# Seven unread identity products beside the first two chains of a delta-rule and feed-forward kernel, and one fold result evicted sooner

## The chip, the cores and the metric

The kernel runs on one core of one Trainium2 chip. The metric is the device time of one execution in microseconds (us). Engines are named as the profile names them: PE is TensorE's matrix product, PEld its weight load, DVE is VectorE, ACT is ScalarE, POOL is GpSimd, SP is SyncE, which here issues nearly all DMAs. PEclk is the share of TensorE's full clock that was granted.

## The reference

Two blocks follow each other. The first is a delta-rule recurrence over 768 steps for 4 batches of 8 heads of 48 features; the second multiplies its output, as 3072 tokens of 384 features, through four weight matrices with no nonlinearity but one product.

```python
k_n = k / (np.linalg.norm(k, axis=-1, keepdims=True) + 1e-06)
for t in range(S):
    kt, vt, bt = (k_n[:, :, t], v[:, :, t], beta[:, :, t, None])
    y[:, :, t] = np.einsum('bhd,bhde->bhe', q[:, :, t], state)
    v_old = np.einsum('bhde,bhd->bhe', state, kt)
    state = state + bt[:, :, :, None] * np.einsum('bhd,bhe->bhde', kt, vt - v_old)
...
a = x @ w1
b = x @ w2
h = a * b @ w3
return (h @ w_out).astype(np.float32)
```

## The kernel before, in words

The 768 steps are cut into 12 chunks of 64. Inside a chunk the recurrence is a triangular system, and chunks are joined by a state. For a chunk m the parts are, by the names in the order string: `k`, `v`, `p` (loads), `d` (transposes into KQ, lines 320 to 330), `s` (scores, lines 357 to 402: products of KQ with itself, L367 and L373, then on VectorE the scaled system U, L379, and the masked PT, L397), `u` (the 32 by 32 blocks of U are written to DRAM, L414), `e` (the corner, lines 476 to 529: two sets of small products at L498, copies at L514, and the evictions into TT at L525), `c` (the chain, lines 543 to 616: S,KQ, then R on VectorE L584, then R,TT, then X L594, then X,ktok, then the new state S at L613 or L615; all four sets of products have the line L551), and `y` (outputs, lines 619 to 687: products L652, copies into xT L673, DMAs within xT L684).

Two chunks share one inverse `V` (lines 420 to 454): their blocks are read back from DRAM as Ub (L426), and 31 pairs of VectorE instructions (L440, L445) invert them; the result goes out as Vd (L453) and comes back into TT (L462, L469) for the corner. The first two inverses work on a pair of PSUM banks, with two ACT copies in (L434) and out (L449).

The weights arrive as 36 pieces `P` of 64-bit words (their two 32-bit halves are put together into one f32 value). A piece is a load (L699), two ACT activations (L707, L708), two VectorE instructions (L710, L711) and one GpSimd addition (L715), with five raw buffers in turn. w3 and w_out are multiplied into one matrix first: `t` transposes (L750, copy L753), `f` folds (lines 756 to 767: eight products L759, the second half in a second step, and an eviction by ACT at L766). Then `a` and `b` (lines 772 to 796, products L779) make the two hidden factors of 512 tokens, `b` for the first of two chunks only, and `S`, `o`, `x` make the result (L846, L874).

Each part is a Python generator. What it does between two `yield`s is one step, and the order string lists the steps one by one; a name's nth appearance is its nth step. Each engine executes its instructions in the order in which the string issues them:

```python
    for name in ORDER.split():
        step(name)
    in_text_order()
```

Two rings of PSUM matter here. `two_banks` (psW) hands out two pairs of banks in turn, to scores, corners, chains and outputs. `bank` (psF) hands out four single banks in turn, to transposes, folds, `a`, `b`, `o` and a few small ones; a product into a bank waits until the bank's last content has been read.

```python
    def bank(shape):
        return in_turn(psF, shape, "f", 4, "ps_f")
```

Around the change the steps are these, in the string's order: first outputs `y0`, scores `s3` for its second pair of batches, the rest of chain `c0` (X,ktok and the first state), transpose `t13`, corner `e1`, chain `c1` (S,KQ, then R,TT), inverse `V1`, the fold `f6`, outputs `y1`, then `b` and `a`.

Of the kernel before, what the change touches and what calls it, by code (L numbers as in the profile page):

```python
# [54 lines left out]
b0 V1 V1 g2 a04 P34 n2 p4 n2 a07 c1 a04 b2 b4 P33 b6 b2 P35 V1 g2 g2 P34 g2 e2 a07 g2 P33 e2
P35 c2 c2 e3 d4 a03 d4 a03 a01 P33 g2 b4 d4 g2 e2 b6 e2 a07 e2 b4 d4 T a01 T b4 e2 a07 c2 s4 p5
g2 c2 T g2 N2 V2 b6 p5 b6 s4 b5 s4 c2 a06 c2 a06 a04 v3 y2 d5 b5 d5 k6 s4 e3 d5 s4 y2 a02 a05
d5 s4 b7 a04 n3 S0 a02 a05 S0 s5 S0 u4 e3 s5 n3 s5 e3 b7 T o0 c3 c3 s5 g3 s5 S0 N2 N2 x0 e3 g3
e3 o0 s5 c3 c3 u5 o0 x0 V2 S0 x0 y3 V2 y3 S0 V2 S0 V2 S0 S0 V2 V2 V2 S0 g3 o0 S0 o0 S0 x0 V2 c3
o0 v4 y3 V2 V2 V2 x0 p6 V2 x0 V2 S0 a10 a10 S0 g3 S0 x0 V2 x0 S0 o0 x0 x0 p6 a14 V2 k7 a17 a17  # L60
a14 V2 V2 V2 a15 a16 V2 a16 a15 V2 g3 V2 V2 V2 V2 V2 v5 V2 x0 a13 V2 V2 V2 a17 a12 V2 a13 g3 V2
V2 g3 a17 c3 a14 a13 d6 d6 a11 V2 e4 n4 a12 e4 e4 c4 d6 V3 e4 a14 a10 n4 g3 d6 c4 e5 a11 e4 s6
g3 a13 e4 a12 p7 a10 c4 g3 N3 s6 c4 s6 a11 y4 n5 y4 c4 e5 a12 c4 a11 a15 c5 n5 e5 p7 a16 d7 d7
d7 d7 o1 c5 v6 a16 k8 g4 g4 e5 g4 p8 a15 g4 s7 s7 S1 e5 s7 S1 e5 x1 s7 s7 S1 s7 c5 o1 s6 S1 u7
c5 o1 s6 s6 u6 S1 S1 V3 S1 y5 c5 c5 V3 V3 V3 V3 V3 o1 S1 x1 k9 S1 y5 S1 y5 o1 S1 S1 x1 x1 V3 S1
S1 V3 c6 V3 S1 S1 V3 d8 o1 x1 x1 v7 a20 n6 x1 V3 a20 o1 x1 a23 V3 V3 x1 V3 x1 n7 a27 a24 d8 a26
V3 V3 V3 V3 x1 g4 V3 a23 V3 a25 V3 a27 a27 V3 a24 V3 V3 a26 a20 V3 g4 V3 p8 V3 V3 V3 V3 p9 V3
V3 a25 d8 n6 d8 g4 a20 a22 a22 a24 V3 c6 a27 a25 a24 a21 a21 e6 e6 e6 g4 e7 N3 e6 a25 N3 g4 s8
g4 N4 s8 e6 a22 s8 a26 e6 c6 c6 N4 s8 a26 s8 y6 a22 V4 p9 N4 S2 d9 e7 s8 a21 e7 y6 u8 d9 a21 e7
c6 a23 d9 p10 e7 d9 S2 c6 S2 s9 n7 a23 s9 e7 o2 s9 c7 s9 S2 s9 k10 S2 c7 x2 o2 c7 S2 S2 o2 u9  # L70
s9 V4 c7 V4 S2 y7 V4 V4 x2 V4 g5 g5 V4 p10 d10 y7 S2 x2 S2 o2 y7 V4 o2 x2 c7 V4 V4 S2 S2 V4 o2
a35 x2 x2 k11 x2 S2 V4 x2 S2 a35 v8 V4 S2 V4 V4 S2 V4 x2 n8 o2 a37 x2 V4 v9 V4 V4 V4 x2 a34 n8
V4 V4 a36 a30 V4 V4 V4 V4 V4 a37 V4 a34 a33 V4 g5 a33 a30 a32 a36 V4 V4 V4 V4 a34 a33 V4 V5 a32
e8 n9 c7 e8 a30 c8 a33 e8 e9 e8 g5 a35 a34 c8 a30 e8 g5 d10 a32 e9 g5 a32 g5 a36 e8 e9 S3 c8
a36 a35 a31 d10 d10 e9 a31 n9 c8 g5 c8 c8 g5 g5 e9 a31 s10 N5 e9 p11 s10 s10 a31 c9 a37 a37 p11
c9 y8 N5 v11 d11 S3 d11 d11 o3 v10 d11 s10 y8 s10 S3 u10 S3 s11 N5 s11 o3 s10 c9 s11 c9 s11 S3
x3 S3 s11 o3 S3 S3 y9 o3 s11 x3 S3 o3 u11 V5 S3 S3 V5 y9 V5 x3 n11 S3 x3 V5 V5 V5 S3 y9 S3 S3
V5 c9 V5 o3 x3 V5 x3 x3 V5 V5 x3 S3 a47 o3 x3 V5 V5 a47 x3 V5 V5 a47 n10 V5 a46 a40 a40 V5 a47
V5 a43 V5 a46 x3 a42 a45 V5 a42 V5 a41 a45 a43 V5 V5 V5 V5 V5 V5 a44 V5 a44 V5 a45 a41 V5 V5 V5
V5 c9 a42 e10 a40 e10 n11 a42 e10 a44 e10 c10 a45 n10 e11 e10 e11 c10 a43 e10 c10 c10 a40 e11  # L80
a41 a46 e11 c10 a44 S4 a43 e11 a41 S4 c10 o4 e11 a46 c11 x4 S4 S4 y10 o4 c11 c11 S4 y10 S4 S4
S4 S4 S4 c11 o4 y11 o4 x4 S4 S4 S4 o4 y11 x4 x4 o4 S4 x4 x4 S4 y11 S4 x4 x4 a50 x4 o4 a50 x4
a55 a56 a55 a52 a55 a50 a52 a56 a54 a57 a54 a55 a54 a50 a54 a51 a52 a57 a51 a53 x4 a52 a53 a51
a56 a56 a53 a51 a53 a57 o5 S5 a57 S5 S5 o5 S5 S5 S5 x5 S5 S5 S5 o5 o5 x5 S5 S5 S5 o5 S5 S5 S5
# [5 lines left out]
def kernel(  # L90
# [14 lines left out]
    P = 128  # L105
# [43 lines left out]
    def bank(shape):  # L149
        return in_turn(psF, shape, "f", 4, "ps_f")  # L150
# [19 lines left out]
    ident = const.tile([P, P], FP32, name="ident")  # L170
# [361 lines left out]
    xts = {}  # L532

    def scaled_v(c):
        nv = vtoks[c]
        for r in range(NR):
            pool.tensor_tensor(  # L537
                out=nv[:, r], in0=nv[:, r],
                in1=scale_of(ns, c)[:, r].unsqueeze(2).to_broadcast([P, H, D]), op=ALU.mult,
            )  # L540
            yield

    def chain(c):
        TT, nv, KQ = TTs[c % 2], vtoks[c], KQs[c]

        def products(out, lhs, rhs):
            ps = two_banks()
            for r in range(NR):
                for h in range(H):
                    for z in range(2):  # L550
                        pe.matmul(  # L551
                            out(ps, r, h, z), lhsT=lhs(r, h, z), rhs=rhs(r, h, z),
                            start=True, stop=True,
                        )
            return ps[:, :, 0:DM].rearrange("p b (g d) -> p b g d", d=D)


        def crossed(ps, r, h, z):
            g = NP * r + h // 2
            return ps[half((z + h) % 2), h % 2, D * g : D * g + D]  # L560

        def by_tokens_of_features(ps, r, h, z):
            g = NP * r + h // 2
            return ps[half(z), h % 2, D * g : D * g + D]

        def by_features(ps, r, h, z):
# [24 lines left out]
        yield
        Xs[c] = X = in_turn(work, [P, NR, H, D], "X", 2, "X")
        for e in range(2):
            dve.tensor_tensor(  # L594
                out=X[:].rearrange("p r (a e) d -> p e (r a) d", e=2)[:, e], in0=ps[:, e],
                in1=scale_of(ws, c, 1).rearrange("p r (a e) -> p e (r a)", e=2)[:, e]
                .unsqueeze(2).to_broadcast([P, H, D]),
                op=ALU.mult,
            )
        yield  # L600
        if c < NCH - 1:
            kt = ktoks[c]
            ps = products(
                by_features,
                lambda r, h, z: kt[half((z + h) % 2), r, h, :],
                lambda r, h, z: X[half((z + h) % 2), r, h, :],
            )
            yield
            Ss[c + 1] = Sn = in_turn(work, [P, 2, H, D], "S", 2, "S")
            for z in range(2):  # L610
                f = feat(z)
                if c == 0:
                    dve.tensor_copy(out=Sn[f], in_=ps[f])  # L613
                else:
                    dve.tensor_tensor(out=Sn[f], in0=St[f], in1=ps[f], op=ALU.add)  # L615
            yield
# [428 lines left out]
```

## Time and profile before

| | us |
|---|---|
| median of 3 runs | 593.02 |
| lowest and highest | 591.44, 594.95 |
| the profiled execution's own time | 593.18 |
| its span, first to last instruction | 591.5 |
| PE busy | 542.2 (92%) |
| DVE busy | 363.0 (61%) |
| ACT busy | 159.3 (27%) |
| POOL busy | 176.3 (30%) |
| mean granted clock of TensorE | 0.976 |

The span is counted from the first to the last instruction of one execution; its own time has some 1.7 us around that. Busy time is a union: products that overlap in the array count once. The chain that ended last is made of 70% PE, 10% SyncE's queue, 9% DMA and 5% DVE. A wait that the profile lists as "issue" is one in which the engine waited for nothing that the profile shows.

### The profile page before, as it was taken

The page shows a single profiled execution, that of the slowest core. Times are in us where ns is not written, and L with a number is a line of the kernel's source. Part 1 is how long each engine was busy: PE and PEld are TensorE (multiplying, and loading weights), DVE is VectorE, ACT ScalarE, POOL GpSimd, SP SyncE. Part 2 cuts the span into 40 slices and gives each one's busy share as a digit, 9 for nine tenths or more (in the row PEclk, how much of TensorE's full clock was granted, in tenths as well). Part 3 has the DMA queues.
Part 4 walks back from the last instruction along what each step waited for, and adds up shares of the span by engine and source line. Part 5 has one row for each costly group of instructions (what it writes and reads, how often), then busy time and mean ns, then how long its engine had stood idle before and what let it go on. Part 6 is the DMA issues. An engine that isn't in the chain of part 4 may idle for free.

```text
span 591.5 us, 19063 instructions
## 1 busy us (share of the span) xinstructions
PE 542.2 (92%) x8188; PEld 379.8 (64%) x8188; DVE 363.0 (61%) x828; ACT 159.3 (27%) x333; POOL 176.3 (30%) x223
## 2 busy tenths in 40 slices
PE   2569898778999999999999989999999999999997
PEld 2466555657878874558854669645698446974477
DVE  3897898569986579574796545865746924110012
ACT  4666354363412202121210232112121112311100
POOL 7563542033464601207121034111170000600051
PEclk9988999679999999999999999999999999999999
DMA  9989986668856455563553345614432040010001
GB/s 245 196 174 267 199 172 130 120 154 169 140 86 98 98 86 111 78 96 54 124 92 79 46 70 103 127 53 66 59 65 90 13 90 4 17 41 13 1 0 53
DMA packets 219507, 57.31 MB, mean 97 GB/s; under 512 B 206656, under 2 KB 212800, under 8 KB 219424
## 3 DMA queue, kind: packets, MB, share of 16 engines
q1 hardware_dynamic: 215232, 55.31, 46.9%
q10 hardware_dynamic: 4192, 0.79, 1.0%
q8 instruction: 64, 1.05, 0.8%
q14 instruction: 19, 0.16, 0.1%
HBM read 43.88 MB, written 11.01 MB: 93 GB/s over the span
## 4 chain that ended last, share of the span: by engine, by line
PE 70%; SPq 10%; DMA 9%; DVE 5%; issue 2%; ACT 1%; POOL 1%; DVEq 0%; POOLq 0%; ACTq 0%
PE ps_f L779 38%; PE ps_f L874 19%; DMA raw<-in_moe_w_dram 5%; PE ps_w L551 5%; PE ps_w L652 4%; SPq L230 3%; SPq L699 2%; PE ps_w L498 2%; DMA ktok<-in_k_dram 2%; DVE tb L440 1%; SPq L202 1%; DVE ps_w L445 1%; PE ps_w L367 1%; DMA Ub<-Ud 1%; PE ps_w L373 1%
## 5 line engine op out<-in xcount | busy, mean ns | idle before, releaser
L779 PE MATMUL ps_f<-xT,w2s 128*128 128x512 f32 (+1 forms) x336 | 131.8, 538 | 2.1 <-issue 2.1
L779 PE MATMUL ps_f<-xT,w1s 128*128 128x512 f32 (+1 forms) x336 | 128.0, 532 | 2.0 <-DMA xT<-xT 2.0
L846 POOL TENSOR_TENSOR ab<-ab 128x256 f32<-128x256 f32 x96 | 67.0, 727 | 175.3 <-DVE ab L795 153.6
L779 PEld LDWEIGHTS ps_f<-xT,w1s 128*128 128x128 f32 x336 | 63.3, 190 | 57.6 <-issue 52.2
L779 PEld LDWEIGHTS ps_f<-xT,w2s 128*128 128x128 f32 x336 | 62.0, 190 | 55.1 <-issue 51.9
L791 ACT COPY ab<-ps_f 128x512 f32<-128x512 f32 (+1 forms) x56 | 28.2, 526 | 165.8 <-PE ps_f L779 161.7
L874 PE MATMUL ps_f<-w,ab 128*128 128x192 f32 x376 | 66.3, 330 | 0.0
L874 PEld LDWEIGHTS ps_f<-w,ab 128*128 128x128 f32 x376 | 61.2, 190 | 4.2 <-issue 3.3
L795 DVE TENSOR_TENSOR ab<-ab,ps_f 128x512 f32<-128x512 f32 (+1 forms) x56 | 33.1, 603 | 48.9 <-PE ps_f L779 48.7
L440 DVE TENSOR_TENSOR tb<-Vb,Ub 128x31 f32<-128x31 f32 (+15 forms) x124 | 44.7, 360 | 17.2 <-DMA Ub<-Ud 13.9
L874 PE MATMUL ps_f<-room,ab 128*128 128x192 f32 x272 | 48.0, 330 | 0.8 <-DVE room L905 0.8
L445 DVE TENSOR_TENSOR Vb<-Vb,tb 128x31 f32<-128x31 f32 (+15 forms) x124 | 46.0, 371 | 4.3
L759 PE MATMUL ps_f<-w2s,w3T 128*128 128x384 f32 x128 | 45.5, 511 | 0.0
L874 PEld LDWEIGHTS ps_f<-room,ab 128*128 128x128 f32 x272 | 44.1, 190 | 1.6 <-issue 1.1
L673 ACT COPY xT<-ps_w 48x256 f32<-48x256 f32 x96 | 30.5, 366 | 54.4 <-PE ps_w L652 53.9
L270 POOL TENSOR_TENSOR sq<-ktok 128x384 f32<-128x384 f32 x24 | 20.7, 866 | 70.0 <-DMA ktok<-in_k_dram 39.5
L759 PEld LDWEIGHTS ps_f<-w2s,w3T 128*128 128x128 f32 x128 | 25.1, 202 | 16.5 <-issue 2.3
L537 POOL TENSOR_TENSOR vtok<-vtok,n 128x384 f32<-128x384 f32 x24 | 20.3, 859 | 43.1 <-DMA vtok<-in_v_dram 43.1
L367 PE MATMUL ps_w<-KQ 48*64 48x128 f32 x384 | 29.3, 293 | 1.7 <-DVE PT L397 1.7
L373 PE MATMUL ps_w<-KQ 48*64 48x64 f32 x768 | 30.1, 232 | 0.0
L715 POOL TENSOR_TENSOR w<-w,raw 128x512 uint32<-128x512 uint32 x16 | 20.6, 1294 | 29.0 <-issue 7.3
L373 PEld LDWEIGHTS ps_w<-KQ 48*64 48x64 f32 x768 | 27.2, 146 | 0.1
(109 smaller groups left out, 661.0 us busy)
## 6 DMA issues: line engine op xcount, KB each, us to landing
raw<-in_moe_w_dram SPq DMA_DIRECT2D x16, 512.0 KB, 6.5
vtok<-in_v_dram SPq DMA_DIRECT2D x24, 192.0 KB, 4.5
raw<-in_moe_w_dram SPq DMA_DIRECT2D x24, 192.0 KB, 4.7
out_dram<-osb SPq DMA_DIRECT2D x46, 96.0 KB, 2.0
ktok<-in_k_dram SPq DMA_DIRECT2D x44, 96.0 KB, 3.6
raw<-in_moe_w_out_dram SPq DMA_DIRECT2D x8, 384.0 KB, 4.4
Ud<-U SPq DMA_DIRECT2D x48, 64.0 KB, 2.6
Ub<-Ud SPq DMA_DIRECT2D x6, 512.0 KB, 4.1
```

What stands on the lines that cost most here:

```text
L367: pe.matmul(ps[half(z), 0, n : n + 128], lhsT=x[:, 0, :], rhs=x.rearrange("p j t -> p (j t)"), start=True, stop=True,)
L373: pe.matmul(ps[half(z ^ j), 1, n + C * j : n + C * j + C], lhsT=x[:, 0, :], rhs=x[:, j, :], start=True, stop=True,)
L440: dve.tensor_tensor(out=tv, in0=V[:, 0 : s + 1, s : s + 1].to_broadcast([P, s + 1, n]), in1=U[:, s, s + 1 : BS].unsqueeze(1).to_broadcast( ...
L445: dve.tensor_tensor(out=o, in0=o, in1=tv, op=ALU.subtract)
L551: pe.matmul(out(ps, r, h, z), lhsT=lhs(r, h, z), rhs=rhs(r, h, z), start=True, stop=True,)
L673: act.copy(out=xT[f, p:NP:2, b : b + NR, cc, :].rearrange("p a r t -> p r a t"), in_=pyv[f, z, b : b + NR],)
L759: pe.matmul(ps[:, 0:DM], lhsT=w3Ts[jc, kc // 4][:, kc % 4 * P : kc % 4 * P + P], rhs=wo[:, kc], start=(kc == 0), stop=(kc == KF - 1),)
L779: pe.matmul(ps[:].rearrange("p b c t -> p b (c t)"), lhsT=w[:, m, js], rhs=x[:, m, :, c0:c1].rearrange("p b c t -> p b (c t)"), start=(m = ...
L791: act.copy(out=t, in_=ps)
L795: dve.tensor_tensor(out=t, in0=t, in1=ps, op=ALU.mult)
L846: pool.tensor_tensor(out=o_, in0=x_, in1=y_, op=op)
L874: pe.matmul(ps[b][:, b, :], lhsT=abs_[u, HF * f + i][:, t0 : t0 + P], rhs=ws_[w][:, i], start=first and i == 0 and (b == 0 or n == "F"), s ...
```

## The change

A new part `fill` has four steps. It takes one psF bank and writes 2, 1, 1 and 3 products of the identity with four copies of itself side by side (128*128 by 128x512) into it. Nothing reads them. The steps stand behind the products of `y0`, behind the second scores of `s3`, behind the second set of the corner `e1`, and behind S,KQ of chain `c1`.

The third step of `f7`, which evicts fold 7 from its bank, moves from behind the thirteenth step of `V1` to behind the first pieces that follow the corner's first products. Since `fill` takes one bank of the ring, every later bank is the next one in turn.

The look-up of a chunk's v tile moves into the lines that use it, in `scaled_v` and in `chain`; the instructions there stay the same.

```diff
-e1 P26 s2 e1 P25 d3 c0 P21 P30 u2 s3 c0 s3 P26 N1 P31 P24 y0 s3 s3 y0 c0 s3 s3 P25 t13 N1 e1 u3
-P31 c0 P26 P31 P32 c1 V1 c1 e1 P25 V1 P27 c1 V1 c1 V1 V1 t13 V1 V1 V1 V1 V1 V1 y0 V1 P25 f7 f6
+e1 P26 f7 s2 e1 P25 d3 c0 P21 P30 u2 s3 c0 s3 P26 N1 P31 P24 y0 fill s3 s3 fill y0 c0 s3 s3 P25
+t13 N1 e1 fill u3 P31 c0 P26 P31 P32 c1 fill V1 c1 e1 P25 V1 P27 c1 V1 c1 V1 V1 t13 V1 V1 V1 V1
+V1 V1 y0 V1 P25 f6 f6 P30 P32 P32 v2 V1 P27 s1 P31 V1 V1 y1 b3 b1 V1 b0 P32 P28 y1 b1 V1 b1 b3
...
     def scaled_v(c):
-        nv = vtoks[c]
...
     def chain(c):
-        TT, nv, KQ = TTs[c % 2], vtoks[c], KQs[c]
+        TT, KQ = TTs[c % 2], KQs[c]
...
-        R = nv
+        R = vtoks.get(c)
...
+    def fill():
+        ps = bank([P, 4, P])
+        for n in (2, 1, 1, 3):
+            for _ in range(n):
+                pe.matmul(
+                    ps[:], lhsT=ident[:], rhs=ident[:].unsqueeze(1).to_broadcast([P, 4, P]),
+                    start=True, stop=True,
+                )
+            yield
...
+    parts["fill"] = fill
```

More of the change, by code (lines that the diff above doesn't have):

```diff
@@ L49 @@
 N1 P30 t12 t14 t15 e0 t15 d3 f7 d3 f6 e0 P30 P21 e0 e0 P24 f7 s2 s2 e1 e0 s2 P24 e0 e1 V1 p4 s2
-e1 P26 s2 e1 P25 d3 c0 P21 P30 u2 s3 c0 s3 P26 N1 P31 P24 y0 s3 s3 y0 c0 s3 s3 P25 t13 N1 e1 u3
-P31 c0 P26 P31 P32 c1 V1 c1 e1 P25 V1 P27 c1 V1 c1 V1 V1 t13 V1 V1 V1 V1 V1 V1 y0 V1 P25 f7 f6
-f6 P30 P32 P32 v2 V1 P27 s1 P31 V1 V1 y1 b3 b1 V1 b0 P32 P28 y1 b1 V1 b1 b3 P29 P27 b2 b3 y1 V1
-P27 b1 b0 P29 P29 c1 a01 b2 a03 P28 V1 a01 a00 b3 P28 P29 a02 a02 a03 P35 P28 V1 a05 b7 a00 V1
-V1 V1 V1 a06 P33 V1 b5 a05 b7 b0 V1 P34 V1 b5 V1 a06 V1 V1 V1 P34 k4 V1 P35 V1 g2 a00 V1 k5 a00
@@ L55 @@
[L55 to L84, printed above, removed]
@@ L85 @@
-o5 x5 S5 x5 o5 x5 x5 x5 x5 x5 x5 x5 x5 x5 x5
+e1 P26 f7 s2 e1 P25 d3 c0 P21 P30 u2 s3 c0 s3 P26 N1 P31 P24 y0 fill s3 s3 fill y0 c0 s3 s3 P25
+t13 N1 e1 fill u3 P31 c0 P26 P31 P32 c1 fill V1 c1 e1 P25 V1 P27 c1 V1 c1 V1 V1 t13 V1 V1 V1 V1
+V1 V1 y0 V1 P25 f6 f6 P30 P32 P32 v2 V1 P27 s1 P31 V1 V1 y1 b3 b1 V1 b0 P32 P28 y1 b1 V1 b1 b3
+P29 P27 b2 b3 y1 V1 P27 b1 b0 P29 P29 c1 a01 b2 a03 P28 V1 a01 a00 b3 P28 P29 a02 a02 a03 P35
+P28 V1 a05 b7 a00 V1 V1 V1 V1 a06 P33 V1 b5 a05 b7 b0 V1 P34 V1 b5 V1 a06 V1 V1 V1 P34 k4 V1
@@ new lines @@
+P35 V1 g2 a00 V1 k5 a00 b0 V1 V1 g2 a04 P34 n2 p4 n2 a07 c1 a04 b2 b4 P33 b6 b2 P35 V1 g2 g2
+P34 g2 e2 a07 g2 P33 e2 P35 c2 c2 e3 d4 a03 d4 a03 a01 P33 g2 b4 d4 g2 e2 b6 e2 a07 e2 b4 d4 T
+a01 T b4 e2 a07 c2 s4 p5 g2 c2 T g2 N2 V2 b6 p5 b6 s4 b5 s4 c2 a06 c2 a06 a04 v3 y2 d5 b5 d5 k6
+s4 e3 d5 s4 y2 a02 a05 d5 s4 b7 a04 n3 S0 a02 a05 S0 s5 S0 u4 e3 s5 n3 s5 e3 b7 T o0 c3 c3 s5
+g3 s5 S0 N2 N2 x0 e3 g3 e3 o0 s5 c3 c3 u5 o0 x0 V2 S0 x0 y3 V2 y3 S0 V2 S0 V2 S0 S0 V2 V2 V2 S0
+g3 o0 S0 o0 S0 x0 V2 c3 o0 v4 y3 V2 V2 V2 x0 p6 V2 x0 V2 S0 a10 a10 S0 g3 S0 x0 V2 x0 S0 o0 x0
@@ new lines @@
+x0 p6 a14 V2 k7 a17 a17 a14 V2 V2 V2 a15 a16 V2 a16 a15 V2 g3 V2 V2 V2 V2 V2 v5 V2 x0 a13 V2 V2
+V2 a17 a12 V2 a13 g3 V2 V2 g3 a17 c3 a14 a13 d6 d6 a11 V2 e4 n4 a12 e4 e4 c4 d6 V3 e4 a14 a10
+n4 g3 d6 c4 e5 a11 e4 s6 g3 a13 e4 a12 p7 a10 c4 g3 N3 s6 c4 s6 a11 y4 n5 y4 c4 e5 a12 c4 a11
+a15 c5 n5 e5 p7 a16 d7 d7 d7 d7 o1 c5 v6 a16 k8 g4 g4 e5 g4 p8 a15 g4 s7 s7 S1 e5 s7 S1 e5 x1
+s7 s7 S1 s7 c5 o1 s6 S1 u7 c5 o1 s6 s6 u6 S1 S1 V3 S1 y5 c5 c5 V3 V3 V3 V3 V3 o1 S1 x1 k9 S1 y5
+S1 y5 o1 S1 S1 x1 x1 V3 S1 S1 V3 c6 V3 S1 S1 V3 d8 o1 x1 x1 v7 a20 n6 x1 V3 a20 o1 x1 a23 V3 V3
@@ new lines @@
+x1 V3 x1 n7 a27 a24 d8 a26 V3 V3 V3 V3 x1 g4 V3 a23 V3 a25 V3 a27 a27 V3 a24 V3 V3 a26 a20 V3
+g4 V3 p8 V3 V3 V3 V3 p9 V3 V3 a25 d8 n6 d8 g4 a20 a22 a22 a24 V3 c6 a27 a25 a24 a21 a21 e6 e6
+e6 g4 e7 N3 e6 a25 N3 g4 s8 g4 N4 s8 e6 a22 s8 a26 e6 c6 c6 N4 s8 a26 s8 y6 a22 V4 p9 N4 S2 d9
+e7 s8 a21 e7 y6 u8 d9 a21 e7 c6 a23 d9 p10 e7 d9 S2 c6 S2 s9 n7 a23 s9 e7 o2 s9 c7 s9 S2 s9 k10
+S2 c7 x2 o2 c7 S2 S2 o2 u9 s9 V4 c7 V4 S2 y7 V4 V4 x2 V4 g5 g5 V4 p10 d10 y7 S2 x2 S2 o2 y7 V4
+o2 x2 c7 V4 V4 S2 S2 V4 o2 a35 x2 x2 k11 x2 S2 V4 x2 S2 a35 v8 V4 S2 V4 V4 S2 V4 x2 n8 o2 a37
@@ new lines @@
+x2 V4 v9 V4 V4 V4 x2 a34 n8 V4 V4 a36 a30 V4 V4 V4 V4 V4 a37 V4 a34 a33 V4 g5 a33 a30 a32 a36
+V4 V4 V4 V4 a34 a33 V4 V5 a32 e8 n9 c7 e8 a30 c8 a33 e8 e9 e8 g5 a35 a34 c8 a30 e8 g5 d10 a32
+e9 g5 a32 g5 a36 e8 e9 S3 c8 a36 a35 a31 d10 d10 e9 a31 n9 c8 g5 c8 c8 g5 g5 e9 a31 s10 N5 e9
+p11 s10 s10 a31 c9 a37 a37 p11 c9 y8 N5 v11 d11 S3 d11 d11 o3 v10 d11 s10 y8 s10 S3 u10 S3 s11
+N5 s11 o3 s10 c9 s11 c9 s11 S3 x3 S3 s11 o3 S3 S3 y9 o3 s11 x3 S3 o3 u11 V5 S3 S3 V5 y9 V5 x3
+n11 S3 x3 V5 V5 V5 S3 y9 S3 S3 V5 c9 V5 o3 x3 V5 x3 x3 V5 V5 x3 S3 a47 o3 x3 V5 V5 a47 x3 V5 V5
@@ new lines @@
+a47 n10 V5 a46 a40 a40 V5 a47 V5 a43 V5 a46 x3 a42 a45 V5 a42 V5 a41 a45 a43 V5 V5 V5 V5 V5 V5
+a44 V5 a44 V5 a45 a41 V5 V5 V5 V5 c9 a42 e10 a40 e10 n11 a42 e10 a44 e10 c10 a45 n10 e11 e10
+e11 c10 a43 e10 c10 c10 a40 e11 a41 a46 e11 c10 a44 S4 a43 e11 a41 S4 c10 o4 e11 a46 c11 x4 S4
+S4 y10 o4 c11 c11 S4 y10 S4 S4 S4 S4 S4 c11 o4 y11 o4 x4 S4 S4 S4 o4 y11 x4 x4 o4 S4 x4 x4 S4
+y11 S4 x4 x4 a50 x4 o4 a50 x4 a55 a56 a55 a52 a55 a50 a52 a56 a54 a57 a54 a55 a54 a50 a54 a51
+a52 a57 a51 a53 x4 a52 a53 a51 a56 a56 a53 a51 a53 a57 o5 S5 a57 S5 S5 o5 S5 S5 S5 x5 S5 S5 S5
@@ L86 @@
+o5 o5 x5 S5 S5 S5 o5 S5 S5 S5 o5 x5 S5 x5 o5 x5 x5 x5 x5 x5 x5 x5 x5 x5 x5
 """
@@ L534, in scaled_v @@
     def scaled_v(c):
-        nv = vtoks[c]
         for r in range(NR):
             pool.tensor_tensor(
-                out=nv[:, r], in0=nv[:, r],
+                out=vtoks[c][:, r], in0=vtoks[c][:, r],
                 in1=scale_of(ns, c)[:, r].unsqueeze(2).to_broadcast([P, H, D]), op=ALU.mult,
@@ L581, in chain @@
             v3, r3 = (
-                x[:].rearrange("p r (a e) d -> p (r a) e d", e=2) for x in (nv, R)
+                x[:].rearrange("p r (a e) d -> p (r a) e d", e=2) for x in (vtoks[c], R)
             )
```

## The prediction

> **What bounds the kernel now.** I read the page's slices first, for the stage: the change sits between the first two chains, at 108 to 123 us of 591.5.
>
> ```profile
> PE   2569898778999999999999989999999999999997
> PEclk9988999679999999999999999999999999999999
> DMA  9989986668856455563553345614432040010001
> ```
>
> TensorE is nearly full from slice 10 (148 us) to the end. Slices 8 and 9 (103 to 133 us) are the one place after 90 us where its granted clock falls, to 0.7 on average, and the DMA engines are busy there. The second view cuts that stretch along the steps of the clock (us; busy us and count of PE, PEld, DVE, ACT, POOL; PEclk; DMA; GB/s):
>
> ```profile
> 105.85:109.26 3.41, 1.38 (x65) 1.12 (x64) 2.05 (x5) 0.33 (x2) 1.28 (x1) 1.00 0.56 67
> 109.27:112.68 3.41, 3.00 (x104) 2.91 (x108) 1.27 (x3) 2.20 (x8) 0.00 (x0) 0.50 0.86 171
> ...
> 119.51:122.92 3.41, 0.51 (x17) 0.54 (x19) 2.65 (x5) 3.30 (x6) 0.00 (x0) 0.50 0.88 198
> 122.92:126.33 3.41, 3.41 (x62) 2.58 (x57) 1.48 (x3) 1.22 (x3) 2.82 (x3) 0.50 1.01 276
> 126.33:129.74 3.41, 3.36 (x102) 2.17 (x100) 2.17 (x9) 1.50 (x3) 2.16 (x2) 1.00 0.24 45
> ```
>
> The clock is halved at 109.27 us, after a window in which TensorE was busy for 1.38 of 3.41 us (40%), and whole again at 126.33 us: 17.06 us at half. In them TensorE is busy for 11.6 us (3.00 + 2.87 + 1.79 + 0.51 + 3.41, two of the five rows not shown).
>
> The timeline of TensorE shows where it waits (start, length, what; idle before, releaser):
>
> ```profile
> 108.42 0.44 PE L652 MATMUL ps_w<-PT,X 64*48 64x64 f32 x15 [1.45 <-issue]
> ...
> 113.65 1.01 PE L750 MATMUL ps_f<-ident,w 128*128 128x128 f32 x4 [0.54 <-issue]
> 114.59 1.13 PE L498 MATMUL ps_w<-T,T 33*33 33x32 f32 x64
> 115.52 1.92 PE L551 MATMUL ps_w<-S,KQ 48*64 48x48 f32 x59
> 118.18 0.45 PE L551 MATMUL ps_w<-S,KQ 48*64 48x48 f32 x5 [0.75 <-issue]
> 122.41 2.08 PE L551 MATMUL ps_w<-R,TT 64*64 64x48 f32 x64 [3.78 <-ACT TT L525]
> 124.42 3.78 PE L759 MATMUL ps_f<-w2s,w3T 128*128 128x384 f32 x8
> 131.96 3.26 PE L779 MATMUL ps_f<-xT,w1s 128*128 128x256 f32 x14 [0.42 <-DMA xT<-xT]
> ```
>
> What those waits hang on decides the case. The longest, 3.78 us before the products of R and TT, is for the corner's evictions (L525, 120.73 to 121.93). On ScalarE these stand behind an activation of a weight piece, and that behind a DMA. The waits of ACT and DVE in 108 to 128 us:
>
> ```profile
> ACT w2s L707 <- DMA raw<-in_moe_w_dram: 4.3, 1, 4.3
> DVE w2s L710 <- ACT w2s L707: 5.1, 1, 5.1
> DVE tb L440 <- DMA Ub<-Ud: 1.7, 1, 1.7
> ```
>
> The chain of waits says the same of what comes next (start, length, what):
>
> ```profile
> 115.14 1.77 SPq L699
> ...
> 121.11 6.09 DMA Ub<-Ud
> ...
> 158.52 3.06 DMA Vd<-Vb
> ...
> 165.20 0.72 DVE T L481
> ```
>
> SyncE's queue is its own bound: the second block load (Ub) is issued at 121.11 us and lands 6.09 us later; inverse 1 on VectorE (L440, L445) starts then, at 127.29, and through Vd ends at the transpose of 165.20, for which TensorE waits 0.93 us. TensorE itself waits for xT at 131.96 (0.42 us) and at 141.59 (1.63 us, not shown), both DMAs that stand in SyncE's order. So **from 109 to 165 us the pace is set by SyncE's queue, the DMAs and VectorE**; TensorE, although slow, arrives early three times.
>
> [...] the clock is half or whole, [...] 0.50 or 1.00 only, and 17.06 us is five times 3.41. [...] here a window 40% busy was enough, while one 1.81 us busy of 3.41 (53%, 139.99 to 143.40 us) kept the whole clock, and one 1.87 us busy of 3.40 (37.6 to 41.0 us) lost it. The border lies near 53 to 55% by this trace. [...]
>
> **The change part by part.**
>
> *Price of a fill.* One product of 128*128 by 128x512 in f32, whose row has a mean of 538 ns from first to last. In a dense stream what counts is the distance: 60 such products take 25.75 us in the chain (217.67 us), 0.43 each. At half clock I take twice that, 0.86. Seven: 3.0 us at whole clock, 6.0 at half. Their weight loads (190 ns each) run beside them. No shown row has the same identity seven times; 0.43 is the low end and 2 x 0.538 = 1.08 (7.5 us in all) the high one.
>
> *Where they stand.* A, two, after the first outputs (L652, end 108.86), where TensorE idles 0.82 us for a VectorE eviction (L397). B, one, after scores r = 1 of chunk 3, before X,ktok: no idle. C, one, after T,T, before S,KQ: no idle at half clock. D, three, after S,KQ, in the 3.78 us.
>
> *If the clock halves as before* (0.86 each): A is 1.72 less 0.82 = 0.90 late; with B 1.76; with C 2.62: S,KQ ends at 118.63 + 2.62 = 121.25, still before VectorE gets to R at 121.36, which had waited for the piece. D runs to 123.83, so R,TT starts 1.42 us after its 122.41. X (L594) then starts near 125.96 instead of 124.54 and ends near 127.0, before the 127.29 at which inverse 1 starts. R,TT had 1.73 us to spare there and uses 1.42. The fold that follows catches up, since more of it lies after 126.33; outputs 1 end about 0.5 late, against 0.42 + 1.63 us of xT waits ahead. **Cost 0.**
>
> *If A holds the clock at 109.27.* A brings 109.27 - 108.86 = 0.41 us more to the window: 1.79 of 3.41, 52%, just below the border of 53 to 55%. If it holds, scores, X,ktok, T,T and S,KQ shrink by some 4 us and A to D cost 3.0, but R,TT still waits for ACT until about 122.4: S,KQ would be over near 116 and D near 117.3, and the 5 us to 122.4 are over a window long, so the clock halves again at 119.5. R,TT starts when it did; **gain 0**. The cover is SyncE's queue, which asks TensorE for nothing here: u3's scores were evicted at 112.45, its issue came at 117.00.
>
> *The eviction of fold 7* (L766, 0.48 us) moves on ScalarE from 123.68 to about 103.2, ahead of one corner's T copies, the first outputs' copies, two pieces, the TT evictions, two copies of Vb and one transpose's copy. At the new place it pushes the T copies (L514) by 0.48; their reader is T,T at 114.59, and ScalarE has 4.55 us idle behind them. At the old place 4.07 us idle follow. Cost 0. It issues no DMA, and SyncE's and GpSimd's orders are as before.
>
> *Banks.* The fills take one of the four psF banks in turn. transpose 13 comes to fold 7's bank (free at about 103.7, needed at 113.65), b3 to fold 6's (128.72 against 130.40), b0 to the fills' own. Nothing waits; later the distances are as before. The look-ups of vtoks change no instruction.
>
> *Sum.* The profiled execution took 593.18 us (span 591.5 and 1.7 around it); 593.18 + 0. The median shown is 0.16 lower, so 593.0.
>
> **The rivals.**
>
> *Faster: TensorE's clock is the bound.* For it: the chain is 70% PE, PE is busy 92%. Half of the 11.6 us, 5.8, would come back, less what isn't covered of the fills (B and C, 0.9): about 588.3. Against it: the three waits above.
>
> *Slower: R,TT passes its 1.73 us to spare.* X is late, inverse 1 starts late on VectorE, and all up to 165 us moves along. It decides once R,TT starts after about 124.1 us. With seven fills at half clock and none covered, 6.0 - 1.73 = 4.3 us: 597.5. For it: my case at half clock leaves just 0.3 us, and each stall of instruction issue (0.54, 0.75, 1.45 us seen here) can shift. Against it: 3.78 us of cover stand ahead of D.
>
> *It doesn't do what it says:* the clock halves all the same; 593, as worked out.
>
> **How the numbers follow.** The time repeats within 591.44 to 594.95 in the runs shown; 0.5% (3.0 us) is about what can be told from no change. No change by 0.5%: 0.79 (with the clock held or not about evenly). Faster rival, over 3.0 us: 0.13. Slower rival, over 3.0 us: 0.08; small slips of inverse 1 lie inside the 0.79. The range takes the shown spread, plus 1.4 us below for a part of the faster case and 0.6 above for a small slip: 590.0 to 595.6.
>
> **What would show it.** Right: R,TT still ends its wait on ACT L525 near 122.4 or behind the fills near 123.8; inverse 1 starts within 0.3 us of 127.3; TensorE still waits for xT and for T L481 at 165; PE busy rises by about 3 us at most. Wrong: TensorE loses those waits, or Ub is issued at another time than 121 us; the transpose of 165.20 moves by over 1 us.

## The result, and the profile after

The changed kernel takes 600.66 us (median of 4 runs, 599.63 to 604.18) against 593.69 us for the kernel before (4 runs, 591.44 to 594.95): 1.0125 times as long, 95% interval 1.0081 to 1.017. (Here and below, ratios and intervals leave out runs of a slower state, over 1.5% above a kernel's fastest, and are not simply the ratios of the medians.) It is slower by some 7 us, where no change was forecast. Its profiled execution took 599.63 us, with a span of 597.9; the span before was 591.5, so the two traces differ by 6.4 us.

The page of the changed kernel: busy share by slice, granted clock, and the queue that brings instructions (transfers, MB, share):

```profile
PE   2469888897999999999999899999999999999997
PEclk9988999997999999999999999999999999999999
...
q8 instruction: 64, 1.05, 0.7%
```

The fills did their own work. The dip of the clock in slices 8 and 9 (0.6 and 0.7 of full speed there before) is gone; the one slice of 0.7 is now slice 10 (134.5 to 149.5 us), and the mean granted clock rose from 0.976 to 0.985. With a better clock the kernel is slower.

The stretch of the fills, cut along the steps of the clock (us; busy us and count of PE, PEld, DVE, ACT, POOL; PEclk; DMA; GB/s), for the changed kernel:

```profile
105.97:109.38 3.41, 1.94 (x76) 1.46 (x69) 2.40 (x4) 0.67 (x3) 1.28 (x1) 1.00 0.73 110
109.39:112.80 3.41, 3.41 (x54) 1.61 (x52) 0.91 (x3) 1.86 (x6) 0.00 (x0) 1.00 1.03 170
...
136.69:140.10 3.41, 1.33 (x67) 0.87 (x65) 1.90 (x5) 1.15 (x3) 1.29 (x1) 1.00 0.13 26
140.11:143.52 3.41, 2.20 (x5) 1.82 (x6) 3.34 (x7) 1.45 (x4) 1.44 (x2) 0.50 0.33 90
143.52:146.93 3.41, 3.41 (x9) 2.70 (x8) 3.14 (x9) 0.37 (x1) 1.13 (x1) 0.50 0.86 222
```

Fill A raises the window that used to lose the clock from 1.38 to 1.94 busy us of 3.41 (57%), and the clock stays whole to 140.11 us. There, behind a window with 1.33 busy us (39%), it halves after all, for two windows, in front of dense work.

The timeline of TensorE in the changed kernel (start, length, what; idle before, releaser; L934 is a fill):

```profile
108.77 1.98 PE L934 MATMUL ps_f<-ident 128*128 128x512 f32 x4
...
111.77 1.12 PE L934 MATMUL ps_f<-ident 128*128 128x512 f32 x2
...
115.21 1.12 PE L934 MATMUL ps_f<-ident 128*128 128x512 f32 x2
...
118.44 2.84 PE L934 MATMUL ps_f<-ident 128*128 128x512 f32 x6
121.51 1.27 PE L550 MATMUL ps_w<-R,TT 64*64 64x48 f32 x64 [0.23 <-issue]
...
141.32 9.05 PE L778 MATMUL ps_f<-xT,w1s 128*128 128x256 f32 x28 [3.30 <-DMA xT<-xT]
```

The counts matter: A is two products and shows four records, D three and six. **An f32 product stands in the trace as two matmul records**, here called passes, each with its weight load: the seven fills are 14 passes and 14 loads, the 28 instructions by which the page's 19091 exceed the 19063 of before.

D ends at 121.28. TT is evicted by 121.04 and R on VectorE (L583) by 121.40, and the products of the two start at 121.51, 0.90 earlier than before, as the weight piece ahead of TT and R landed 0.9 earlier. The fills are out of the way 0.12 us before R. TensorE does not wait where it waited 0.42 us for xT before; at the next wait for xT it stands 3.30 us instead of 1.63. Up to there the change costs nothing. The loss lies behind it. The waits of TensorE from 166 us to the end, put down to issue (who and whose line; us in total, times, longest), in the kernel before:

```profile
PE ps_f L779 <- issue: 2.1, 1, 2.1
PE ps_w L498 <- issue: 0.5, 1, 0.5
```

and in the changed kernel:

```profile
PE ps_w L550 <- issue: 2.4, 2, 1.4
PE ps_w L498 <- issue: 2.0, 2, 1.6
...
PE ps_w L651 <- issue: 1.2, 2, 1.0
```

Their places, from the changed kernel's timeline:

```profile
285.09 0.24 PE L550 MATMUL ps_w<-X,ktok 64*48 64x48 f32 x1 [0.98 <-issue]
...
332.43 0.26 PE L498 MATMUL ps_w<-T,T 33*33 33x32 f32 x5 [1.61 <-issue]
...
348.47 0.39 PE L550 MATMUL ps_w<-X,ktok 64*48 64x48 f32 x14 [1.44 <-issue]
...
513.54 0.32 PE L651 MATMUL ps_w<-KQ,S 48*48 48x64 f32 x5 [1.04 <-issue]
```

The same places in the kernel before:

```profile
282.52 0.91 PE L551 MATMUL ps_w<-X,ktok 64*48 64x48 f32 x64
...
328.20 0.76 PE L498 MATMUL ps_w<-T,T 33*33 33x32 f32 x64
...
345.47 1.98 PE L779 MATMUL ps_f<-xT,w2s 128*128 128x512 f32 x4 [2.05 <-issue]
```

Groups of 64 that ran through before are now cut in two by a wait that no engine and no DMA of data ends; one wait of 2.05 us is gone. With every issue wait of over 0.1 us after 166 us added up, the kernel before has 3.8 us of them and the changed one 6.8. Some 1.2 us of each sum are ten waits of 0.12 us, all ahead of an output's products, which both kernels have.

Setting the same pass side by side in both traces, fills left out, gives the account of the 6.4 us. The changed kernel is 1.87 us early at 139, 2.5 late at 144 and 1.50 late at 166 (the hole before xT and the half clock, less what the wait for T L481 takes up). At 194 it gets 0.72 back, where an issue wait of before is gone. Then it loses 1.10 at 283, 1.84 at 329, 1.70 less 2.08 at 343 to 345, 0.58 at 418, 0.41 at 427, 0.83 at 449 (a wait for room in a bank, ended by VectorE) and 1.27 at 507. So **issue waits make 4.1 us, the stretch of the clock at 140 us 1.5, the bank 0.8**.

**Where the issue waits stand.** Number TensorE's passes in the trace from 0. From 100 us on, the issue waits of over 0.15 us stand at passes 978, 1105, 1232, 1359, 2626 and 5038 in the kernel before, and at 1105, 1359, 1485, 4277, 4657, 5038, 6179, 6433 and 7701 in the changed one (but for the 0.23 us ahead of R,TT, which starts behind R): the distances are multiples of 127, or one to three passes short of one. The queue "instruction" of the page moves 1.05 MB in 64 transfers, each of 16384 bytes. In the kernel before its transfers start at 101.5, 105.7, 110.5 and 115.2 us, and the issue waits end at 104.26, 108.42, 113.65 and 118.18, 2.7 to 3.1 us later. At all the waits listed for the two kernels the first pass follows 2.2 to 3.1 us behind the start of a transfer. That the queue is TensorE's shows in its count too: 64 transfers in every kernel here of up to 8202 passes, 65 in every one of 8216 or more. So TensorE's program comes in packets, one for each 127 passes with their loads by the distances above. The author's reading, an estimate from these numbers, is that **a border between two packets costs a wait when the passes ahead of it are used up before the next packet has come**: where the passes still left when the transfer starts last less than those 2.2 to 3.1 us. The start itself varies: 0.5 to 2.1 us behind the border before in the kernel before, but 6.7 us behind it for the packet of pass 1485 in the changed one. Short products in a row are used up soonest: the chain's group of 64 passes at 282.52 us in the kernel before took 0.91 us. Of long ones, at 0.43 us a pass, five to seven cover 2.2 to 3.1 us (an estimate from these numbers).

### The profile page after: what moved, and what is told of

It reads as the page before. It is cut to its first block, busy times and chain, and to the rows that moved or that the text cites. A ratio compares the mean times of both kernels' runs of the same rounds, so it can differ in the third digit from the quotient of the medians.

```text
span 597.9 us, 19091 instructions
## 1 busy us (share of the span) xinstructions
PE 547.6 (92%) x8202; PEld 380.1 (64%) x8202; DVE 361.8 (61%) x828; ACT 159.5 (27%) x333; POOL 176.1 (29%) x223
## 3 DMA queue, kind: packets, MB, share of 16 engines
q8 instruction: 64, 1.05, 0.7%
## 4 chain that ended last, share of the span: by engine, by line
PE 72%; DMA 11%; DVE 7%; SPq 5%; issue 3%; ACT 1%; POOL 0%; ACTq 0%; DVEq 0%; POOLq 0%
PE ps_f L778 41%; PE ps_f L873 17%; PE ps_w L550 5%; DMA raw<-in_moe_w_dram 4%; PE ps_w L651 4%; PE ps_w L498 3%; DMA Ub<-Ud 2%; SPq L230 2%; SPq L414 1%; DVE tb L440 1%; PE ps_w L367 1%; DVE ps_w L445 1%; DMA vtok<-in_v_dram 1%; PE ps_w L373 1%; DMA Ud<-U 1%
## 5 line engine op out<-in xcount | busy, mean ns | idle before, releaser
L778 PE MATMUL ps_f<-xT,w1s 128*128 128x512 f32 (+1 forms) x336 | 130.5, 542 | 3.3 <-DMA xT<-xT 3.3
L778 PEld LDWEIGHTS ps_f<-xT,w1s 128*128 128x128 f32 x336 | 65.3, 196 | 59.3 <-issue 51.4
L758 PE MATMUL ps_f<-w2s,w3T 128*128 128x384 f32 x128 | 44.2, 500 | 0.2 <-ACT w3T L752 0.2
L614 DVE TENSOR_TENSOR S<-S,ps_w 48x768 f32<-48x768 f32 x20 | 19.0, 950 | 14.2 <-PE ps_w L550 12.3
```

Of the source, the lines that this page charges most:

```text
L758: pe.matmul(ps[:, 0:DM], lhsT=w3Ts[jc, kc // 4][:, kc % 4 * P : kc % 4 * P + P], rhs=wo[:, kc], start=(kc == 0), stop=(kc == KF - 1),)
L778: pe.matmul(ps[:].rearrange("p b c t -> p b (c t)"), lhsT=w[:, m, js], rhs=x[:, m, :, c0:c1].rearrange("p b c t -> p b (c t)"), start=(m = ...
```

## The experiments

Three theories. **Fetch**: the fills' 28 instructions move every later packet border by 14 passes, and borders fall inside groups of short products; only the number of added instructions counts, modulo a packet, not their length or what they do to the clock. **Clock**: the half clock at 140 us, taken to be brought on by TensorE coming early, is the loss. **Bank**: the psF bank that `fill` takes, or fold 7's earlier eviction, shifts later buffers. In the diffs `wide` is the change's product of 128*128 by 128x512; `narrow` is a product of the identity's corner, 64*64 by 64x16, with nobody to read it, of two short passes. e1 to e4 are compared with the same 13 runs of the kernel before, e5 to e8 with 56, e9 to e12 with 67; e2, e3 and e4 have four runs each, the others 10 to 22.

**The bank and the eviction without the products** (e1_bank; the four steps of `fill` and the moved step of `f7` stay in ORDER).

```diff
-        for n in (2, 1, 1, 3):
+        for n, m in zip((0, 0, 0, 0), (0, 0, 0, 0)):
```

> The change without its products: the bank is taken, fold 7 is evicted sooner, nothing is issued to TensorE. Three theories of the 6.4 us by which the changed execution is longer. Clock: TensorE held at full clock arrives sooner, waits 3.3 us for xT at 138, and the clock halves there, in front of dense work (+2.8 us by 144, +1.5 left at 166). Fetch: TensorE's instructions come in packets of 16 KB (64 in the profile), the seven products are 14 weight loads and 14 passes more and move every later packet border by 14 passes; borders that fall into runs of short products cost a wait called issue (+4.1 us in sum after 166). Bank: the shifted ring and the moved eviction cost. Clock and fetch both expect the time of the kernel before, within 1 us; bank expects up to 600.

Measured: 593.91 us against 592.71, 1.004 (1.0012 to 1.0069). Its issue waits after 166 us are 3.0 us. Some 8 of the 12 thousandths of the change need the products; whether the other 4 are real this run leaves open. Run again below. Its trace also bears on the clock (columns as above):

```profile
140.46:143.87 3.41, 1.24 (x4) 0.61 (x5) 2.79 (x6) 2.47 (x5) 1.30 (x1) 1.00 0.13 29
143.87:147.28 3.41, 3.41 (x9) 2.78 (x9) 3.17 (x9) 0.37 (x1) 1.29 (x1) 0.50 0.89 240
```

Without a single fill product, and with TensorE only 0.12 us ahead of the kernel before at 139 us, the clock halves behind the window that holds most of the wait for xT (2.78 us here), in front of the same products. So the half clock at 140 us does not need the fills, and its 1.5 us in the changed kernel's trace cannot be put down to them on this evidence.

**Seven short products in the same places** (e2_narrow7).

```diff
-        for n in (2, 1, 1, 3):
+        for n, m in zip((0, 0, 0, 0), (2, 1, 1, 3)):
...
+            for k in range(m):
+                narrow(ps, k)
```

> The change with its seven products cut to 64*64 by 64x16, in the same places: the same 14 weight loads and 14 passes, next to no activity. Fetch expects the issue waits of the changed kernel after 250 us (0.98, 1.61, 1.44, 1.04 near the same places) and some +4 to +5 us over before, with the clock halved from about 109 to 126 us as before. Clock expects the time of before, within 1 us.

Measured: 602.21 us, 1.0163 (1.0102 to 1.0225). As slow as the change or slower, 9.5 us where fetch expected 4 to 5, though these products take next to no time (0.38 us for four of their passes at 118.70 us) and R,TT behind them takes 2.08 us, as at the half clock of the kernel before, and not the 1.27 of the changed one. Its issue waits after 166 us add up to 7.3 us, 1.25 at 283, 1.87 at 330 and 1.44 near 350 among them, the change's own places. Count, not length, then. Its windows (columns as above) show one thing more:

```profile
327.80:331.27 3.47, 2.46 (x179) 2.23 (x168) 2.39 (x14) 1.65 (x3) 0.00 (x0) 1.00 0.62 83
331.27:338.10 6.83, 5.84 (x12) 2.68 (x12) 2.25 (x7) 1.18 (x2) 0.00 (x0) 0.50 0.22 28
```

The clock halves for 6.83 us at 331.27, in the middle of the issue wait of 330.4 to 332.3 us, and the trace loses 4.7 us between 329 and 344. It halves again at 351.75, 0.4 us behind the wait near 350, and in e4 and e6 at 0.4 to 1.4 us behind waits of 1.6 to 2.6 us. So a fetch that comes late seems able to cost twice. That the wait does it is not shown: the window that ended at 331.27 was busy for 2.46 of 3.47 us, and the 2.05 us at 345 in the kernel before left the clock whole.

**The clock held at 140 us as well** (e3_hold): seven more products of the identity, 128*128 by 128x256, ahead of the first ab product of (u, jc, c0) = (0, 1, 1), in its own bank.

```diff
             ps = bank([P, B, c1 - c0, C])
+            if (u, jc, c0) == (0, 1, 1) and w is w1s:
+                pv = ps[:].rearrange("p b c t -> p (b c t)")
+                for _ in range(7):
+                    hold(pv)
```

> The change, and seven more identity products of 128*128 by 128x256 in the bank of the first product that waits for xT at 138 us (7 x 0.43 = 3.0 us into a wait of 3.3). The clock should then stay whole at 140. Clock expects the 2.8 us between 141 and 144 to come back, so 1.5 us at 166, and if clock is all, 594. Fetch expects that all but that stays: the border is moved by 28 passes in place of 14, which by the distances between borders in the trace of before (an estimate: a wait where 127 passes take under 3.3 us) costs as much as 14 does, so about 599 against 600.5 of the change.

Measured: 605.54 us, 1.0275 (1.0204 to 1.0346), in spite of a whole clock from 113.75 us on (mean 0.991, the best of all kernels here). Slower than the change by 5 us, with issue waits of 9.6 us after 166 us: the border has now moved by 28 passes. The clock theory asked for a gain; fetch named the right side, but not the size: it expected 599. In the trace, 10.0 us longer than before's, 2.4 us are there by 166 us and 7.6 come after; why the median lies higher still is open.

**Twenty short products, no long one** (e4_narrow20), at the place of D: 40 passes.

```diff
-        for n in (2, 1, 1, 3):
+        for n, m in zip((0, 0, 0, 0), (0, 0, 0, 20)):
```

> No wide product; twenty of 64*64 by 64x16 in the place of the last three, in the wait for ACT TT. 40 passes in place of 14. Fetch expects the worst place of all by the same estimate: 7.5 us of issue waits more than before (11.1 against 3.7), so 598 to 603, with no change of the clock at 140. Clock expects the time of before, within 1 us.

Measured: 608.25 us, 1.0291 (1.0247 to 1.0335), more than either theory gave. Its waits from 166 us on that are put down to issue:

```profile
PE ps_w L550 <- issue: 4.8, 3, 2.6
PE ps_w L498 <- issue: 3.0, 2, 1.6
PE ps_w L373 <- issue: 2.7, 2, 1.6
PE ps_w L651 <- issue: 1.6, 2, 0.8
```

Up to 2.6 us for one wait, 13.2 us for all: the loss follows these waits.

If fetch is right, enough added instructions, a whole packet, should take the loss away. That is the test of the next runs. All of them put narrow products into the wait for the second k tile, at 12 to 16 us, where TensorE idles; N is the number of products.

```diff
         ps = [bank([P, NR, NP, C]) for z in range(2)]
+        if (m, i) == (1, 0):
+            for x in range(N):
+                y = x % 2
+                pe.matmul(
+                    ps[0][half(y), 0, 0, 0:16], lhsT=ident[half(y), half(y)],
+                    rhs=ident[half(y), 0:16], start=True, stop=True,
+                )
```

**The change with 57 of them** (e5_change_aligned): 114 passes and the fills' 14 make 128, about one packet.

> The change, and 57 products of 64*64 by 64x16 in TensorE's wait for the second k tile at 12 to 16 us. With the seven wide ones they are 128 weight loads and 128 passes, [...] so behind the second chain each packet border stands where it stood before the change. Fetch expects the late issue waits of before (0.54 in a corner near 194, 2.05 near 343, none near 283, 331, 513), and what is left is the clock at 140 to 147: 1.5 us over before at 166, 593 to 596 in all. Against fetch: still some 7 us over before.

Measured: 595.41 us against 593.68, 1.0031 (1.0004 to 1.0058). Three quarters of the loss are gone by adding 114 passes to the changed kernel. The issue waits after 166 us fall from 6.8 to 3.3 us. The longest stands where it stood in the kernel before (1.70 at 344); the 0.54 at 194 is gone, and there is one of 0.40 at 263. In this profiled execution the clock did not halve at 140 us either, so the remaining 0.3% is not put down to one or the other.

**Before with 7** (e7_before_7): 14 passes, no fill, no moved eviction; ORDER as before.

> The kernel before, with seven narrow products in the wait at 12 to 16 us and nothing else, no bank and no eviction moved: every later border stands 14 passes earlier in the program, as behind the fills of the change. Fetch expects the late issue waits of the changed kernel (near 283, 329, 343, 428, 507 of the trace of before) and 4 to 9 us over before. Clock and bank expect the time of before, within 1 us.

Measured: 600.24 us, 1.0113 (1.0078 to 1.0149). **Fourteen short passes at 12 us cost what the change costs**, with the stretch of the fills untouched. In its trace, with the clock whole from 128 us on as in the kernel before, 5.7 us are lost behind 166 us. Its timeline shows the waits at the change's places (L558, L505 and L659 are the change's L550, L498 and L651):

```profile
283.25 0.24 PE L558 MATMUL ps_w<-X,ktok 64*48 64x48 f32 x1 [0.86 <-issue]
...
330.64 0.26 PE L505 MATMUL ps_w<-T,T 33*33 33x32 f32 x5 [1.67 <-issue]
...
347.00 0.24 PE L558 MATMUL ps_w<-X,ktok 64*48 64x48 f32 x1 [1.44 <-issue]
...
511.22 0.32 PE L659 MATMUL ps_w<-KQ,S 48*48 48x64 f32 x5 [1.05 <-issue]
```

**Before with 60** (e6_before_60): 120 passes, some eight short of a packet, picked as the best place by the distances.

> The kernel before, with 60 such narrow products in the wait at 12 to 16 us and nothing else: every later border stands 120 passes earlier in the program, or 8 later. By the distances between borders in the trace of before (an estimate as above) that leaves 2.5 us of issue waits where before has 4.5 and the change 6.9. Fetch expects 2 us less than before, 590 to 592; against fetch: the time of before, or more by what of the 60 products' 3 to 4 us isn't covered.

Measured: 594.53 us, 1.0007 (0.9984 to 1.003). No gain: a miss for the finer use of the theory. In the profiled execution (598.65 us, well above its median) an issue wait of 1.79 us at 496 and the half clock after it stand in the way.

**The change, four holds and 49 early** (e8_hold4_aligned): 8 + 14 + 98 = 120 passes, hold as in e3 with four products.

> The change with four identity products of 128*128 by 128x256 in the bank of the first product that waits for xT at 138 us (1.7 us of a wait of 3.3), and 49 narrow products in the wait at 12 to 16 us, 120 passes in all. Clock and fetch together expect the clock whole at 140 and the borders of the kernel with 60: no loss at 141 to 144 and fewer issue waits, 2 to 4 us under before, 589 to 591. If the hold doesn't pay, the time of the kernel with 60; if the borders don't matter, 598 to 600.

Measured: 595.35 us, 1.0012 (0.9988 to 1.0037). A miss for the gain expected here. In its trace nothing is lost at 141 to 144 us and it stands 0.13 us ahead of the kernel before at 166; but the clock was at half from 118.47 to 125.29 us, so it is no trial of a whole clock through the stage. The trace of e5 comes nearer: whole from 114.47 us on, and at 166 us it stands 0.41 us behind the kernel before. A whole clock from there on gains nothing, which fits the prediction's own ground, that SyncE's queue, the DMAs and VectorE set the pace there.

**The bank again** (e9_bank_again, the kernel of e1) and **the eviction alone** (e10_f7_only):

```diff
-e1 P26 s2 e1 P25 d3 c0 P21 P30 u2 s3 c0 s3 P26 N1 P31 P24 y0 s3 s3 y0 c0 s3 s3 P25 t13 N1 e1 u3
-P31 c0 P26 P31 P32 c1 V1 c1 e1 P25 V1 P27 c1 V1 c1 V1 V1 t13 V1 V1 V1 V1 V1 V1 y0 V1 P25 f7 f6
+e1 P26 f7 s2 e1 P25 d3 c0 P21 P30 u2 s3 c0 s3 P26 N1 P31 P24 y0 s3 s3 y0 c0 s3 s3 P25 t13 N1 e1
+u3 P31 c0 P26 P31 P32 c1 V1 c1 e1 P25 V1 P27 c1 V1 c1 V1 V1 t13 V1 V1 V1 V1 V1 V1 y0 V1 P25 f6
```

> The change without its products once more (bank taken, fold 7 evicted sooner), against a first look of 1.004 [1.0012, 1.0069]. If the ring or the eviction costs anything it comes again, 1.003 to 1.005; if that look was the spread of runs, 0.998 to 1.002.

> The kernel before with the eviction of fold 7 moved and nothing else. By the prediction's step (0.48 us of an idle ScalarE at both places) and by fetch: 1.000 within 0.002. If the eviction is what costs in the kernel without products, 1.003 to 1.005 here too, and the ring is free.

Measured: e9 593.34 us against 594.37, 0.9983 (0.9961 to 1.0005); e10 594.2 us, 1.0003 (0.9976 to 1.0031). The bank and the eviction cost nothing that can be told, and the bank theory falls. e1 and e9 are one kernel, 593.91 and 593.34 us; it was mostly the kernel before that moved, from 592.71 to 594.37. Their intervals do not meet, so a difference of 0.4% here can come from the runs it was compared with.

**Before with 64** (e11_before_64): 128 passes, about one whole packet, nine times as many as in e7.

> The kernel before with 64 narrow products in the wait at 12 to 16 us: one whole packet, so every later border stands where it stood. Fetch expects the late issue waits of before (2.05 near 343, none near 283, 331, 513) and its time, plus what of the 64 products isn't covered, 0 to 1.5 us: 1.000 to 1.003. If TensorE's instructions cost by their number and not by the place of the borders, more than the seven narrow products did, over 1.011.

Measured: 594.71 us against 594.37, 1.001 (0.999 to 1.0029). This decides it: 14 passes in one place cost 1.1%, 128 in the same place nothing that can be told. The banks and the order of work are the same in both kernels; what differs is the number of added passes, and with it where the borders fall. The places say the same: in the change, e2, e3, e4 and e7 long waits stand at passes 4277, 4657, 5038 and 7701 (4658 and 7702 in e3), although e3 and e4 have moved the products on by 14 and 26 passes more. Its waits from 166 us on that are put down to issue are again one at ab and little else (L786 is L779 of before):

```profile
PE ps_f L786 <- issue: 1.4, 1, 1.4
PE ps_w L558 <- issue: 0.4, 1, 0.4
```

and the group that stood at 345.47 us before waits there once more, after an X,ktok group that is whole:

```profile
345.97 0.94 PE L558 MATMUL ps_w<-X,ktok 64*48 64x48 f32 x64
...
348.33 2.84 PE L786 MATMUL ps_f<-xT,w2s 128*128 128x512 f32 x6 [1.43 <-issue]
```

**Before with 49** (e12_before_49): 98 passes.

> The kernel before with 49 narrow products there: borders 98 passes earlier, by the estimate from the distances between borders one of the two best places (2.7 us of issue waits against 4.5 in before and 2.5 with 60 products, which measured 1.0007 in place of 0.997). Fetch expects 0.996 to 1.001; the estimate is rough, as the 60 products showed a wait of 1.8 us near 496 that it had not.

Measured: 596.34 us, 1.0035 (1.0013 to 1.0057), above what was expected. The distances between borders rank the places roughly; they do not price them. One reason may be that the start of a packet's transfer varies, as shown above.

All kernels in one table (issue waits of over 0.1 us and time at half clock are sums of one profiled execution each):

| kernel | ratio, 95% | issue waits after 166 us | half clock after 136 us |
|---|---|---|---|
| before | 1 | 3.8 | 0 |
| change, +14 passes | 1.0125 (1.0081 to 1.017) | 6.8 | 6.8 |
| e7, +14 early | 1.0113 (1.0078 to 1.0149) | 8.0 | 0 |
| e2, +14 short | 1.0163 (1.0102 to 1.0225) | 7.3 | 10.2 |
| e3, +28 | 1.0275 (1.0204 to 1.0346) | 9.6 | 0 |
| e4, +40 | 1.0291 (1.0247 to 1.0335) | 13.2 | 6.8 |
| e12, +98 | 1.0035 (1.0013 to 1.0057) | 4.1 | 3.4 |
| e6, +120 | 1.0007 (0.9984 to 1.003) | 3.7 | 3.4 |
| e8, +120 | 1.0012 (0.9988 to 1.0037) | 3.6 | 0 |
| e5, +128 | 1.0031 (1.0004 to 1.0058) | 3.3 | 0 |
| e11, +128 | 1.001 (0.999 to 1.0029) | 3.0 | 3.4 |
| e1, +0 | 1.004 (1.0012 to 1.0069) | 3.0 | 3.4 |
| e9, +0 | 0.9983 (0.9961 to 1.0005) | 3.3 | 0 |
| e10, +0 | 1.0003 (0.9976 to 1.0031) | 2.6 | 3.4 |

The third column orders the ratios roughly (up to 4.1 us: at most 1.004; 6.8 to 8.0: 1.011 to 1.016; more: 1.0275 and up), though it does not price them; the fourth does not (e3 and e7 lose with a whole clock, e6 and e11 lose nothing with a window at half).

What stays open: the 0.3% of e5, no more than e1 and e9 differ by; how often the clock halves at 140 us in runs without a profile, and so its share in the median; and the wait for room near 449 us, which takes 0.4 to 1.7 us in eight of the 14 traces, e1's among them, and is missing in the others, e9's among them. None of these kernels beats the kernel before.

## Why the prediction was wrong, point by point

**What bounds the stage: right up to the wait for xT at 138 us.** R,TT starts at 121.51, behind R and not behind the fills, and near the 122.4 worked out; that it is 0.90 sooner is the weight piece's DMA. Inverse 1 starts at 124.75, 2.5 us earlier than before, since Ub was issued at 120.33 and landed sooner; TensorE makes nothing of it and waits for xT. The changed kernel's own clock is whole from 75.25 to 140.11 us, and TensorE, 1.87 us early at 139, only waits longer: the faster rival falls there. Behind it, with the half clock, TensorE comes late: VectorE's transpose for it is done at 166.34, and the products of T and U start at 167.55.

**That A tips the window: right in kind.** 1.94 of 3.41 us kept the clock, where 1.79 was worked out and called just below the border. The border itself stands on little: the prediction's own windows have 1.81 us that kept the clock and 1.87 that lost it, and in e2 one busy for 2.46 of 3.47 us lost it.

**The price of a fill: mis-sized by two.** The 60 records in 25.75 us were passes, not products. A, B, C and D took 1.98, 1.12, 1.12 and 2.84 us at whole clock, 7.1 us in sum and not 3.0. The upper bound, 7.5, held it. It did no harm: scores r = 1 came 1.0 us late, and the cover ahead of R,TT took the rest, to the last 0.12 us.

**The waits for issue: the step that failed.** The prediction named them ("each stall of instruction issue (0.54, 0.75, 1.45 us seen here) can shift") and priced the shift only where the fills stand, against 3.78 us of cover. The shift has no end: all later borders move by 14 passes, into 400 us of dense work with no cover. e7 measures that term alone: 1.0113, some 6.7 us of the change's 7. The view that would have shown it was at hand, TensorE's waits after 166 us and the numbers of the passes at which they stand. The slower rival had the right sign and the wrong mechanism: R,TT was not late.

**"The clock halves again": place not foreseen.** It was expected at 119.5 us, under cover. It came at 140.11, in the 3.30 us for xT and in front of dense products; the stretch costs 1.5 us of the 6.4 in the profiled execution. TensorE's coming early makes that wait longer, but e1 and e11, 0.12 us early and 1.28 late at 139 us, lose the clock in a wait at the same place. Its moment differs from trace to trace: the half clock starts at 140.11, 143.87 (e1) and 144.80 us (e11), and between 136 and 160 us in no other trace here, that of e9, the kernel of e1, among them.

**The bank and fold 7's eviction at nothing: right** (e9 and e10).

**What would show it** worked in part. The wait for xT came as written, and R,TT within a microsecond. Inverse 1 started 2.5 us early, where 0.3 was allowed, and PE busy rose by 5.4 us, where 3 was. The transpose of 165.20 moved by 0.43 only, short of the mark of "wrong":

```profile
165.63 0.71 DVE L481 STREAM_TRANSPOSE T<-TT 128x512 f32<-128x512 f32 x1
```

The mark that was met is the lost wait for T L481: TensorE comes to the products behind it 1.50 us later than before. Ub went out at 120.33 us, 0.8 earlier, which did no harm. All the marks lay before 166 us, and most of the loss after it.

## What to carry to other kernels

An edit that adds instructions to a full engine moves every later border between its instruction packets (here one for each 127 passes of TensorE; 14 passes more cost 1.1% in e7): before costing it, list that engine's issue waits over the whole run, number the instructions at which they stand, and see what the shift brings into groups of short products. Where an edit loses by about the same amount wherever it is put, try it with a whole packet of idle instructions at a place that waits anyway; if the loss goes (from 1.25% to 0.31% in e5), it was the border and not the edit. An engine that is brought to its next wait sooner gains nothing by itself: TensorE, 1.87 us early at 139 us, waited 3.30 us for xT in place of 1.63. Before a trace's loss is put down to a change, look for the same loss in a kernel that leaves the change out, as e1 does.

## What the runs showed of the hardware

- TensorE's instructions came in 64 transfers of 16384 bytes (before and the change), one for each 127 passes with their loads by the distances of the issue waits. A border cost up to 2.6 us (e4) or nothing. 14 added passes cost 1.1%, 40 cost 2.9%, 128 about nothing.
- An f32 product was recorded as two passes, each with a load (the seven fills as 14 and 14); one of 128*128 by 128x512 took 0.95 to 1.12 us at whole clock.
- The clock halved behind windows of 3.41 us that were busy for 1.14 (e11), 1.24 (e1), 1.33 (the change) and 1.38 us (before), and stayed whole behind one of 1.94 (the change). The busy time alone does not decide: it also halved behind 2.46 of 3.47 us (e2, 331.27 us).
